# First stage of a pooled-attention and two-MLP kernel: conversion chains, softmax reload and query loads laid out over other steps

## The chip, the cores and the metric

One core of a Trainium2 chip runs the whole program. The metric is the device time of one execution in microseconds (us). Engines are called as the profile calls them: PE (matmul), PEld (its weight loads), DVE, ACT, POOL, and SP, whose queue issues every DMA here.

## The reference, cut to what matters

```python
k_p = k.reshape(B, H, Sp, 8, D).mean(axis=3)      # keys and values pooled by 8: 576 -> 72 rows
v_p = v.reshape(B, H, Sp, 8, D).mean(axis=3)
attn = softmax(q @ k_p.T / sqrt(D))               # B = H = 8, 576 queries, D = 64
x = (attn @ v_p) as 4608 tokens x 512
h = x @ w_in;  x = (h * sigmoid(h)) @ w_out       # first MLP, d_ff 2048
h = x @ w_in2; out = (h * clip(h + 3, 0, 6) / 6) @ w_out2
```

The weights arrive as 64-bit floats and the product must keep more than one 32-bit matmul pass gives. So each weight is converted from its two 32-bit words, and then split into a high part and a remainder (two tiles in the matmul's format).

## The kernel before, in words

Tokens are worked in 9 groups of 512 (`NG`), each of 4 tiles of 128 (`TPG`). The first stage is a loop over 9 groups times 16 blocks of d_ff: step n = 16 g + f. Each step makes one block of h in `h_mm` (12 matmuls of 128x512: high and remainder parts of 4 blocks of depth), and beside it pieces of other chains, at places that tables fix:

- **Attention of a later tile** (table `todo`): `scores`, one step later `all_exps` (row maximum on DVE, eight exponentials with row sums on ACT), later `norm`, then either `probs_T` (group 1: transposes on PE) or `vector_T` (transposes of 32x32 on DVE, then through DRAM: `move` stores the block `bl` and reloads it re-ordered), `weighted` (product with the pooled values) and `split_x` (high part on ACT, remainder on DVE).
- **Conversion of w_in**, in group 0 alone: `split_a` (scale on ACT, shift, merge of the low word and sign on DVE) and `split_b` (high part on ACT, remainder on DVE), called by `conv_a` and `conv_b` after a step's matmuls, about five and four steps ahead of use. For every other weight block (`mul`) the sign is an activation on ACT (L116) and a multiplication on POOL (L125) in place of the third DVE instruction (L127).
- **Factors of later stages** (`pair_jobs`, groups 1 to 8): pairs of weight quarters are loaded (`load_half`), converted (`half_a`), combined on POOL (`combine`), split (`half_b`, tile `hout`) and stored. One job is run per step by `run_job`, 7 jobs a pair, none at f in `REST`.
- **Pooling of keys and values** (`pool_k`, `pool_v`): on POOL, but for the first keys of batch 0 and all of batch 1, which DVE reduces (L336).
- **silu** of the step before: tanh on ACT, one multiply-add on DVE, store of g.

`manual_schedule` keeps each engine's instructions in the order in which the program writes them, so one instruction that waits holds up all behind it on that engine; that goes for SP's queue of DMAs too. In a step the order is: loads, everything in `later` (stores of g and of factors, `move`), silu, `split_x`, softmax, `h_mm`, scores or weighted, conversions or a factor job, norm and turn, pooling. Buffers that matter: 2 for q tiles, 4 PSUM banks for h in turn (so `h_mm(n)` needs the silu of step n - 4), 2 PSUM banks for scores, 3 raw quarters, 4 converted quarters (`mag`), 4 split ones (`out`).

The first stage ends at 559 us; the two later stages are the same code in both kernels.

Of the kernel before, what the change touches and what calls it, by code (L numbers as in the profile page):

```python
# [25 lines left out]
def kernel(  # L26
# [80 lines left out]
    def split_a(f, mul=False):  # L107


        raw = w_raw.pop(f)  # L110
        hw = raw[:, :, 1]
        mag = prep_tile("out", [P, DM], F32)
        bits = mag.bitcast(U32)
        nc.scalar.activation(mag, hw.bitcast(F32), AF.Copy, scale=2.0 ** -112)
        if mul:
            nc.scalar.activation(hw.bitcast(F32), hw.bitcast(F32), AF.Sign)  # L116
        nc.vector.tensor_scalar(
            out=bits, in0=bits, scalar1=3, scalar2=None, op0=ALU.logical_shift_left
        )
        nc.vector.scalar_tensor_tensor(  # L120
            out=bits, in0=raw[:, :, 0], scalar=29, in1=bits,
            op0=ALU.logical_shift_right, op1=ALU.bitwise_or,
        )
        if mul:
            nc.gpsimd.tensor_tensor(out=mag, in0=mag, in1=hw.bitcast(F32), op=ALU.mult)  # L125
        else:
            nc.vector.scalar_tensor_tensor(  # L127
                out=bits, in0=hw, scalar=0x80000000, in1=bits,
                op0=ALU.bitwise_and, op1=ALU.bitwise_or,
            )  # L130
        w_mag[f] = mag

    def split_b(f):

        mag = w_mag.pop(f)
        t = wts.tile([P, 2, DM], F32R, tag=f"i{f}", name="whl")
        nc.scalar.activation(t[:, 0, :], mag, AF.Copy)
        nc.vector.tensor_tensor(out=t[:, 1, :], in0=mag, in1=t[:, 0, :].bitcast(F32), op=ALU.subtract)
        t = t.rearrange("p a (c f) -> p a c f", f=P)
        w_sl[f] = (t[:, 0], t[:, 1])  # L140
# [64 lines left out]
    def factor_jobs():  # L205

        rest = []
        for piece, n in ((2, NF // 2), (0, EARLY)):
            for p in range(n):
                yield from pair_jobs(p, piece, rest)  # L210
        yield None, rest

# [40 lines left out]
    def pair_jobs(p, piece, rest):  # L253
        d, j = divmod(p, 2)
        m = half_mag
        a11, a12, a21, a22 = quarters(p, piece)

        def out(k, key):
            return lambda: half_b(m[key], piece, d, k, j)

        def make(op, to, x, y):
            return lambda: combine(op, m[to], m[x], m[y])

        first, rest[:] = list(rest), [out(1, a12)]
        return [
            (a22, first),
            (a21, [out(3, a22)]),

            (a11, [make(ALU.add, a22, a21, a22), out(4, a22)]),
            (a12, [out(0, a11)]),  # L270
            (None, [make(ALU.subtract, a21, a11, a21), out(6, a21), make(ALU.subtract, a22, a22, a11)]),
            (None, [out(5, a22), make(ALU.subtract, a22, a12, a22)]),
            (None, [out(2, a22)]),
        ]


# [84 lines left out]
    den_t = {}  # L361
    pT_t = {}
    xs = {}

    def load_q(t, tag=None):
        qt = staging(tag, DM) if tag else att.tile([P, DM], F32, tag="q", name="qT")
# [71 lines left out]
    def all_exps(t):  # L438

        mx = att.tile([P, H, 1], F32, tag="mxa", name="mxa")  # L440
# [4 lines left out]
        nc.vector.tensor_scalar(out=mx, in0=mx, scalar1=-ESCALE, scalar2=None, op0=ALU.mult)  # L445
        for h in range(H):
# [41 lines left out]
    def vector_T(t):  # L488
# [12 lines left out]
        def move():  # L501
            nc.sync.dma_start(out=blocks[t % 2], in_=bT)
            rows = blocks[t % 2].rearrange("(i r) j h q -> j r i (h q)", r=Q)
            for j in range(NB):
                n = min(Q, SP - j * Q)
                nc.sync.dma_start(
                    out=pT[j * Q:j * Q + n].rearrange("r i h q -> r i (h q)"), in_=rows[j, :n]
                )

        later.append(move)  # L510
# [256 lines left out]
    with tc.manual_schedule():  # L767
# [16 lines left out]
        for j in range(NPAIR):  # L784
            load_k(1, j, f"o{NF - 8 + j}")
        for j in range(NPAIR):
# [16 lines left out]
        ]  # L803
        conv = list(range(NF))
        done = []

        def conv_a(n, mul):
            for i in range(n):
                if conv:
                    done.append(conv.pop(0))  # L810
                    split_a(done[-1], mul=(i < mul))

        def conv_b(n=9):
            for _ in range(min(n, len(done))):
                split_b(done.pop(0))

# [28 lines left out]
        conv_a(1, 0)  # L845
# [4 lines left out]
        conv_b(1)  # L850
# [4 lines left out]
        conv_a(2, 2)  # L855
        conv_b(1)
        conv_a(2, 2)
        conv_b(1)
        load_ahead(6)

        REST = (0, 3, 6, 13)
        jobs = list(factor_jobs())
        ahead2 = [key for key, _ in jobs if key]
        jobs_b = []
# [11 lines left out]
        def run_job():  # L876

            nonlocal jobs_b
            for job in jobs_b:
                job()  # L880
            key, jobs_b = jobs.pop(0) if jobs else (None, [])
            if key:
                half_a(*key)

        late_silu = []
        pv = {}
        for g in range(NG):
# [3 lines left out]
            for f in range(NF):  # L891
                n = g * NF + f
                load_ahead(2)
                if n == 2:
                    load_q(TPG)
                if g:
                    load_halves()
                while later:
                    later.pop(0)()
                if late_silu:  # L900
                    silu(*late_silu.pop())
                for what, t in todo.get(n, ()):
# [354 lines left out]
```

## Time and profile before

| | us |
|---|---|
| median of 3 runs | 1589.53 (1588.78 to 1590.38) |
| the profiled execution | 1589.21 |
| its span, first to last instruction | 1586.9 |
| PE busy | 1514.5 (95%) |
| DVE / ACT / POOL busy | 1244.2 / 788.9 / 361.2 |

A share of busy time is a mean over stages. The first stage fills the first third of the span, and PE's idle time lies there. Where a view says `x <- y`, x waited and y was what ended the wait.

### The profile page before, as it was taken

Reading aid. Unit: us, or ns where it says so; the run is one execution under the profiler, and the core shown is the slowest. Engines: PE = TensorE matmul, PEld = TensorE weight load, DVE = VectorE, ACT = ScalarE, POOL = GpSimd, SP = SyncE. Lnnn points to the kernel's source line nnn. Section 1 sums busy time; section 2 is a strip of 40 time slices with the busy share of each in tenths; the row PEclk is TensorE's granted clock in tenths of the full one; section 3 lists DMA queues with packets and bytes.
Section 4 is the critical chain, followed back from the end, with each engine's and each line's share of the span. In section 5 each row is a group of like instructions: output and inputs, shape, how many; then the busy total and the mean of one; then the engine's idle time right before and its main releaser. Section 6 shows DMA issues by size and latency. Waiting matters only on the chain.

```text
span 1586.9 us, 31188 instructions
## 1 busy us (share of the span) xinstructions
PE 1514.5 (95%) x11870; PEld 1433.9 (90%) x11870; DVE 1244.2 (78%) x1795; ACT 788.9 (50%) x1689; POOL 361.2 (23%) x405
## 2 busy tenths in 40 slices
PE   7679799899999999999999999999999999999998
PEld 6468688777788899999999999999999999999998
DVE  7776777687677588998888699888885877878776
ACT  5454454445455344444434466776766534334342
POOL 4455144343401000010000044554543000000000
PEclk9789999999999999999999999999999999999999
DMA  9337777787878985555545956666757954444440
GB/s 295 137 91 220 242 256 252 239 267 226 264 263 272 393 299 192 186 190 176 173 133 183 399 187 216 241 216 214 250 197 262 373 220 134 142 150 146 148 149 32
DMA packets 184820, 342.17 MB, mean 216 GB/s; under 512 B 17120, under 2 KB 89696, under 8 KB 184672
## 3 DMA queue, kind: packets, MB, share of 16 engines
q1 hardware_dynamic: 184672, 340.20, 63.1%
q8 instruction: 93, 1.52, 0.4%
q14 instruction: 55, 0.45, 0.1%
HBM read 194.90 MB, written 145.23 MB: 214 GB/s over the span
## 4 chain that ended last, share of the span: by engine, by line
PE 71%; DVE 12%; DMA 9%; ACT 4%; issue 2%; POOL 1%; SPq 1%; ACTq 0%; DVEq 0%; POOLq 0%
PE pl L729 21%; PE pl L713 21%; PE hps L555 11%; PE px L652 9%; PE pz L652 4%; PE py L652 2%; DMA bl<-stage 2%; ACT pr L448 2%; DVE g L569 2%; DVE hmag L172 1%; DMA wraw<-in_moe_w_in_dram 1%; DMA g<-g 1%; DVE go L1098 1%; DMA hraw<-in_moe_w_out_dram 1%; DVE hmag L169 1%
## 5 line engine op out<-in xcount | busy, mean ns | idle before, releaser
L555 PE MATMUL hps<-x,whl 128*128 128x512 f32 x1728 | 402.9, 392 | 9.6 <-ACT x L536 5.6
L555 PEld LDWEIGHTS hps<-x,whl 128*128 128x128 f32 x1728 | 331.7, 195 | 63.5 <-ACT x L536 6.3
L699 ACT ACTIVATE gs<-gr 128x1024 fp32r<-128x1024 f32 x252 | 253.2, 1053 | 262.3 <-issue 109.2
L713 PEld LDWEIGHTS pl<-gs,wst 128*128 128x128 f32 x3024 | 337.8, 192 | 0.1
L729 PE MATMUL pl<-wst,gs 128*128 128x256 f32 x3024 | 337.8, 275 | 0.0
L713 PE MATMUL pl<-gs,wst 128*128 128x256 f32 x3024 | 337.8, 275 | 0.0
L729 PEld LDWEIGHTS pl<-wst,gs 128*128 128x128 f32 x3024 | 337.8, 192 | 0.0
L700 DVE TENSOR_TENSOR gs<-gr,gs 128x1024 fp32r<-128x1024 f32 x252 | 298.0, 1224 | 36.8 <-ACT gs L699 36.2
L652 PE MATMUL px<-xst,wst 128*128 128x256 f32 x1728 | 206.5, 276 | 5.3 <-ACT c L1163 3.4
L652 PEld LDWEIGHTS px<-xst,wst 128*128 128x128 f32 x1728 | 199.3, 192 | 6.7 <-ACT c L1163 4.0
L201 POOL TENSOR_TENSOR hmag<-hmag 128x256 f32<-128x256 f32 x96 | 82.2, 860 | 455.2 <-DVE hout L196 390.0
L692 DVE TENSOR_TENSOR gr<-gr 128x1024 f32<-128x1024 f32 x144 | 169.5, 1218 | 0.0
L448 ACT ACTIVATE pr<-aps,mxa 128x72 f32<-128x72 f32 x256 | 78.1, 330 | 139.1 <-DVE mxa L445 139.1
L196 DVE TENSOR_TENSOR hout<-hmag,hout 128x256 fp32r<-128x256 f32 x152 | 83.4, 556 | 64.2 <-ACT hout L192 60.4
L569 DVE SCALAR_TENSOR_TENSOR g<-g,hps 128x512 f32<-128x512 f32 x144 | 97.1, 675 | 39.1 <-ACT g L568 38.0
L568 ACT ACTIVATE g<-hps 128x512 f32<-128x512 f32 x144 | 85.7, 610 | 67.1 <-PE hps L555 62.1
L629 POOL TENSOR_TENSOR xst<-xr,xst 128x512 fp32r<-128x512 f32 x58 | 81.3, 1402 | 135.5 <-ACT xst L624 131.3
L652 PE MATMUL pz<-xst,wst 128*128 128x256 f32 x864 | 109.3, 276 | 1.4 <-POOL xst L629 0.9
L652 PEld LDWEIGHTS pz<-xst,wst 128*128 128x128 f32 x864 | 102.5, 192 | 2.3 <-POOL xst L629 1.5
L192 ACT ACTIVATE hout<-hmag 128x256 fp32r<-128x256 f32 x152 | 62.7, 420 | 56.6 <-POOL hmag L201 37.0
L399 PE MATMUL aps<-kbd,qT 128*128 128x144 f32 (+1 forms) x288 | 44.5, 311 | 33.0 <-DMA qT<-in_q_dram 16.0
L399 PEld LDWEIGHTS aps<-kbd,qT 128*128 128x128 f32 (+1 forms) x288 | 36.6, 188 | 41.5 <-ACT pr L448 13.0
(87 smaller groups left out, 1515.4 us busy)
## 6 DMA issues: line engine op xcount, KB each, us to landing
gr<-g SPq DMA_DIRECT2D x144, 512.0 KB
ws<-hout SPq DMA_DIRECT2D x152, 256.0 KB
wst<-ws SPq DMA_DIRECT2D x76, 512.0 KB
g<-g SPq DMA_DIRECT2D x144, 256.0 KB
g<-go SPq DMA_DIRECT2D x144, 256.0 KB
hraw<-in_moe_w_out_dram SPq DMA_DIRECT2D x64, 256.0 KB
bl<-stage SPq DMA_DIRECT2D x28, 384.0 KB
stage<-in_k_dram SPq DMA_DIRECT2D x32, 288.0 KB
```

The source lines that it names most:

```text
L196: nc.vector.tensor_tensor(out=t[:, 1], in0=mag, in1=t[:, 0].bitcast(F32), op=ALU.subtract)
L201: nc.gpsimd.tensor_tensor(out=out, in0=a, in1=b, op=op)
L448: nc.scalar.activation(p_t[t][:, a, i], s_t[t][a][:, i], AF.Exp, scale=ESCALE, bias=mx[:, h], accum_out=den_of(t)[:, h],)
L555: nc.tensor.matmul(ps, w[:, c, :], shuffled(x[:, c, :]), start=(c == 0 and n == 0), stop=(c == NKC - 1 and n == 2),)
L568: nc.scalar.activation(in_two(t), dealt(ps), AF.Tanh)
L569: nc.vector.scalar_tensor_tensor(out=in_two(t), in0=in_two(t), scalar=1.0, in1=dealt(ps), op0=ALU.add, op1=ALU.mult)
L652: nc.tensor.matmul(ps[:, j * HW:(j + 1) * HW], w[:, j, a, c, :], shuffled(x[:, b, c, :]), start=(first and j == 0 and n == 0 and c == 0), ...
L692: nc.vector.tensor_tensor(out=to, in0=a, in1=b, op=ALU.subtract)
L699: nc.scalar.activation(t[:, dd, 0], src, AF.Copy)
L700: nc.vector.tensor_tensor(out=t[:, dd, 1], in0=src, in1=t[:, dd, 0].bitcast(F32), op=ALU.subtract)
L713: nc.tensor.matmul(ps[:, c * HW:(c + 1) * HW], w[:, b, c * P:(c + 1) * P], shuffled(t[:, dd, a, i]), start=(dd == 0 and c == 0 and i == 0 ...
L729: nc.tensor.matmul(ps[:, c * HW:(c + 1) * HW], t[:, dd, a, i, c * P:(c + 1) * P], shuffled(w[:, b]), start=(dd == 0 and c == 0 and i == 0 ...
```

## The change

The order of the work within a step of the first stage, and over how many steps a chain is spread:

- **w_in conversion** becomes four functions: `split_scale` (ACT) five steps ahead of use, `split_bits` (three DVE instructions) four steps ahead, `split_head` (ACT) and `split_tail` (DVE) three steps ahead, the tail behind the step's matmuls, the others ahead of them. No block uses the sign activation and the POOL multiplication any more.
- **Softmax**: the maxima (`all_max`) come first in the step, ahead of silu; the exponentials last ahead of the matmuls, behind the conversion's and the factor job's ACT pieces.
- **Factor pairs** take eight slots in place of seven jobs; scale, bits, head and tail of one quarter lie in different slots, ACT and the first DVE pieces ahead of the matmuls, tails and POOL's combinations behind them. They start at step 14 in place of 16, rest at two blocks of a group in place of four, and so end at step 132 (loads start at step 10).
- **Softmax reload**: the store of `bl` (`there`) is issued one step after the turn, as before; its reload (`back`) one step after that for tiles 8 to 11 and two steps after it from tile 12 on. Both stand ahead of the step's other stores.
- **q** has 3 buffers, and is loaded two tiles ahead. Batch 1's keys are pooled by POOL ahead of the loop. Loads of later keys and values move from the end of a step to its start.

```diff
-    def split_a(f, mul=False):
+    def split_scale(f):
+        hw = w_raw[f][:, :, 1]
+        mag = w_mag[f] = prep_tile("out", [P, DM], F32)
+        nc.scalar.activation(mag, hw.bitcast(F32), AF.Copy, scale=2.0 ** -112)
...
+    def split_bits(f):
...
-        if mul:
-            nc.scalar.activation(hw.bitcast(F32), hw.bitcast(F32), AF.Sign)
...
-        if mul:
-            nc.gpsimd.tensor_tensor(out=mag, in0=mag, in1=hw.bitcast(F32), op=ALU.mult)
-        else:
-            nc.vector.scalar_tensor_tensor(
-                out=bits, in0=hw, scalar=0x80000000, in1=bits,
+        nc.vector.scalar_tensor_tensor(
+            out=bits, in0=raw[:, :, 1], scalar=0x80000000, in1=bits,
...
+    def split_head(f):
+        t = w_sl[f] = wts.tile([P, 2, DM], F32R, tag=f"i{f}", name="whl")
+        nc.scalar.activation(t[:, 0, :], w_mag[f], AF.Copy)
+    def split_tail(f):
...
+        def first(i):
+            if i == 0:
+                half_scale(*a22)
+            elif i == 1:
+                half_scale(*a21)
+                half_bits(*a22)
+            elif i == 2:
+                head(3, a22)
+                half_scale(*a11)
+                half_bits(*a21)
...
+        def second(i):
+            if i == 2:
+                tail(3, a22)
+                make(ALU.add, a22, a21, a22)
...
+            elif i == 7:
+                tail(2, a22)
+        return [(first, second, i) for i in range(8)]
...
-        later.append(move)
+        at_slot(n + 1, there)
+        at_slot(n + (2 if t < 3 * TPG else 3), back)
...
+        for j in range(NPAIR):
+            pool_k(1, j, nc.gpsimd)
...
-        REST = (0, 3, 6, 13)
+        REST = (0, 6)
...
-                if g:
+                if n in (0, 1):
+                    load_q(TPG + 1 + n)
+                if n >= NF - 6:
                     load_halves()
+                if n in kv_in:
+                    load_k(*kv_in[n])
+                    load_v(*kv_in[n])
+                for job in due.pop(n, ()):
+                    job()
                 while later:
                     later.pop(0)()
+                for what, t in now:
+                    if what == "soft":
+                        all_max(t)
                 if late_silu:
                     silu(*late_silu.pop())
...
+                if n + 3 < NF:
+                    split_head(n + 3)
+                if n + 4 < NF:
+                    split_bits(n + 4)
+                if n + 5 < NF:
+                    split_scale(n + 5)
+                job = jobs.pop(0) if n >= NF - 2 and f not in REST and jobs else None
+                if job:
+                    job[0](job[2])
+                for what, t in now:
+                    if what == "soft":
                         new_pr(t)
                         all_exps(t)
                 ps = h_mm(g, f)
...
-                        if t + 1 < NTILE:
-                            load_q(t + 1)
+                        if TPG < t + 2 < NTILE and t > TPG:
+                            load_q(t + 2)
...
-                if g == 0:
-                    conv_b()
-                    conv_a(1, f % 2)
-                elif f % 2 == 0 if g == NG - 1 else f not in REST:
-                    run_job()
...
+                if n + 3 < NF:
+                    split_tail(n + 3)
+                if job:
+                    job[1](job[2])
```

PE's own order is the same in both kernels. Three places on the engines beside it, as the program's order lists them (the line numbers of the change are its own; `hout` is the converted weight in group 0, `whl` its split form, `aps` the scores, `mxa` the maxima, `pr` the probabilities):

DVE, group 0, the step in which tile 4's maxima are taken. Before, from a conversion's shift on:

```order
L117 TENSOR_SCALAR hout<-hout 128x512
L120 SCALAR_TENSOR_TENSOR hout<-wraw,hout 128x512
L127 SCALAR_TENSOR_TENSOR hout<-wraw,hout 128x512
L569 SCALAR_TENSOR_TENSOR g<-g,hps 128x512
L442 TENSOR_REDUCE mxa<-aps 128x4 x2
L445 TENSOR_SCALAR mxa<-mxa 128x8
L138 TENSOR_TENSOR whl<-hout,whl 128x512
```

Now, that step from its start:

```order
L474 TENSOR_REDUCE mxa<-aps 128x4 x2
L477 TENSOR_SCALAR mxa<-mxa 128x8
L613 SCALAR_TENSOR_TENSOR g<-g,hps 128x512
L118 TENSOR_SCALAR hout<-hout 128x512
L121 SCALAR_TENSOR_TENSOR hout<-wraw,hout 128x512
L125 SCALAR_TENSOR_TENSOR hout<-wraw,hout 128x512
L137 TENSOR_TENSOR whl<-hout,whl 128x512
```

The maxima moved ahead of silu and of the step's conversion.

ACT at the same place. Before, the exponentials of tile 4 and the next step:

```order
L448 ACTIVATE pr_89,den<-aps,mxa 128x72 x8
L137 ACTIVATE whl<-hout 128x512
L114 ACTIVATE hout<-wraw 128x512
L116 ACTIVATE wraw<-wraw 128x512
L568 ACTIVATE g<-hps 128x512
```

Now the step with tile 4's exponentials:

```order
L612 ACTIVATE g<-hps 128x512
L132 ACTIVATE whl<-hout 128x512
L111 ACTIVATE hout<-wraw 128x512
L484 ACTIVATE pr_89,den<-aps,mxa 128x72 x8
L612 ACTIVATE g<-hps 128x512
```

The high part `whl`, for which DVE's remainder waits, moved from behind the exponentials to ahead of them, and the sign activation is gone.

SP in group 1, around the softmax block of one tile. Before:

```order
L502 DMA bl_101<-stage 128x768
L506 DMA stage<-bl_101 32x4x256 x2
L506 DMA stage<-bl_101 8x4x256
L573 DMA g_1_187<-g 128x2x256
L367 DMA qT<-in_q_dram 128x512
```

Now:

```order
L543 DMA bl_101<-stage 128x768
L617 DMA g_1_187<-g 128x2x256
L199 DMA ws_0_3_161<-hout 128x512
L154 DMA hraw<-in_moe_w_out_dram 128x512
L549 DMA stage<-bl_101 32x4x256 x2
L549 DMA stage<-bl_101 8x4x256
```

Between the store and the reload that waits for it, the stores and the load of the next step moved in.

## Rows read from the trace of the kernel before

**Rows 1.** The page's head

```profile
span 1586.9 us, 31188 instructions
```

**Rows 2.** Windows: us; PE, PEld, DVE, ACT, POOL busy; clock, DMA share, GB/s

```profile
31.00:125.30 94.30, 67.02 (x344) 53.25 (x345) 71.04 (x104) 49.65 (x130) 45.48 (x49) 0.84 0.42 135
125.30:512.20 386.90, 359.91 (x2066) 304.62 (x2065) 284.28 (x614) 188.15 (x714) 126.51 (x188) 0.97 0.77 250
512.20:559.00 46.80, 46.80 (x219) 41.00 (x218) 23.74 (x43) 17.31 (x34) 3.65 (x5) 1.00 1.01 381
```

**Rows 3.** Waits of PE, 31 to 125.3: us in total, times, longest

```profile
PE aps L399 <- ACT pr L448: 7.0, 3, 6.2
PE aps L480 <- DVE pr L469: 6.2, 3, 3.0
PE aps L399 <- DMA qT<-in_q_dram: 4.6, 1, 4.6
...
```

**Rows 4.** Waits of PE, 110 to 560

```profile
PE aps L399 <- DMA qT<-in_q_dram: 11.4, 6, 4.2
PE hps L555 <- ACT x L536: 4.8, 1, 4.8
PE aps L520 <- DMA stage<-bl: 4.5, 2, 2.6
PE aps L399 <- POOL kbd L331: 3.2, 2, 2.2
...
```

**Rows 5.** Timeline of PE: start, duration, work, idle before

```profile
189.86 4.54 PE L555 MATMUL hps<-x,whl 128*128 128x512 f32 x12 [4.78 <-ACT x L536]
...
512.18 46.89 PE L555 MATMUL hps<-x,whl 128*128 128x512 f32 x216
```

**Rows 6.** Waits of all engines, 31 to 125.3

```profile
ACT pr L448 <- DVE mxa L445: 15.0, 4, 6.2
DVE whl L138 <- ACT whl L137: 14.1, 6, 3.2
ACT whl L137 <- POOL hout L125: 12.9, 8, 4.4
```

**Rows 7.** Groups by line: count, busy us, mean ns, idle before

```profile
L125 POOL TENSOR_TENSOR hout<-hout,wraw 128x512 f32<-128x512 f32 x9 | 12.0, 1338 | 53.7 <-ACT g L568 29.4 <-DVE hout L120 22.9 <-ACT whl L137 1.4
...
L336 DVE TENSOR_REDUCE kbd<-stage 64x72 f32<-64x576 f32 x14 | 10.4, 746 | 5.6 <-DMA stage<-in_k_dram 5.5
...
L127 DVE SCALAR_TENSOR_TENSOR hout<-wraw,hout 128x512 uint32<-128x512 uint32 x7 | 7.3, 1040 | 0.2
```

**Rows 8.** Groups by line: pooling of keys on POOL

```profile
L326 POOL TENSOR_TENSOR stage<-stage 128x288 f32<-128x288 f32 x25 | 21.7, 868 | 75.4 <-DMA stage<-in_k_dram 75.4
...
L331 POOL TENSOR_TENSOR kbd<-stage 64x72 f32<-64x72 f32 x50 | 18.2, 364 | 3.4
...
L327 POOL TENSOR_TENSOR stage<-stage 128x144 f32<-128x144 f32 x25 | 12.5, 501 | 2.0
```

**Rows 9.** Timeline of DVE, one instruction alone and one beside POOL

```profile
50.19 0.69 DVE L120 SCALAR_TENSOR_TENSOR hout<-wraw,hout 128x512 uint32<-128x512 uint32 x1
...
55.79 1.64 DVE L120 SCALAR_TENSOR_TENSOR hout<-wraw,hout 128x512 uint32<-128x512 uint32 x1
```

**Rows 10.** Timeline of POOL at that place

```profile
55.43 1.44 POOL L346 TENSOR_TENSOR stage<-stage 72x512 f32<-72x512 f32 x1
```

**Rows 11.** Waits of SP's queue, 125 to 512

```profile
SPq L506 <- DMA bl<-stage: 114.6, 28, 6.6
```

**Rows 12.** Waits of all engines, 125 to 512

```profile
ACT pr L448 <- DVE mxa L445: 124.2, 28, 8.6
...
DVE hout L196 <- ACT hout L192: 59.3, 23, 3.0
```

**Rows 13.** Chain that ended last, in order of time: start, us, what

```profile
126.80 4.54 DMA hraw<-in_moe_w_out_dram
...
422.02 6.16 DMA qT<-in_q_dram
```

More of the change, by code (lines that the diff above doesn't have):

```diff
@@ L203 @@
     EARLY = 5
[L205 to L211, printed above, removed]
     def quarters(p, piece):
@@ L365, in load_q @@
     def load_q(t, tag=None):
[L366 removed]
+        qt = staging(tag, DM) if tag else att.tile([P, DM], F32, tag="q", name="qT", bufs=3)
         nc.sync.dma_start(out=qt, in_=q[t])
@@ L436, in max_exps, with all_max @@
         s_t.pop(t)
-    def all_exps(t):
-        mx = att.tile([P, H, 1], F32, tag="mxa", name="mxa")
+    def all_max(t):
+        mx = mx_t[t] = att.tile([P, H, 1], F32, tag="mxa", name="mxa")
         for a in range(2):
@@ L499, in vector_T, with there, back @@
             )
-        def move():
+        def there():
             nc.sync.dma_start(out=blocks[t % 2], in_=bT)
+        def back():
             rows = blocks[t % 2].rearrange("(i r) j h q -> j r i (h q)", r=Q)
             for j in range(NB):
-                n = min(Q, SP - j * Q)
+                m = min(Q, SP - j * Q)
                 nc.sync.dma_start(
-                    out=pT[j * Q:j * Q + n].rearrange("r i h q -> r i (h q)"), in_=rows[j, :n]
+                    out=pT[j * Q:j * Q + m].rearrange("r i h q -> r i (h q)"), in_=rows[j, :m]
                 )
-        later.append(move)
+        at_slot(n + 1, there)
+        at_slot(n + (2 if t < 3 * TPG else 3), back)
         pT_t[t] = lambda h, o, n: pT[:, o // Q:(o + n) // Q, h, :]
@@ L854 @@
         split_x(3, pv3)
[L855 to L858, printed above, removed]
-        load_ahead(6)
-        REST = (0, 3, 6, 13)
-        jobs = list(factor_jobs())
-        ahead2 = [key for key, _ in jobs if key]
-        jobs_b = []
+        split_bits(1)
+        split_scale(2)
+        split_head(1)
+        split_bits(2)
+        split_tail(1)
+        split_scale(3)
+        split_head(2)
+        split_bits(3)
+        split_tail(2)
+        split_scale(4)
+        load_ahead(6)
+        REST = (0, 6)
+        jobs = []
+        pairs = [(p, 2) for p in range(NF // 2)] + [(p, 0) for p in range(EARLY)]
+        ahead2 = []
+        for p, piece in pairs:
+            jobs += pair_slots(p, piece)
+            ahead2 += [quarters(p, piece)[i] for i in (3, 2, 0, 1)]
         w_need = [(d, k) for k in LAST[2:] for d in range(ND)]
@@ L953 @@
         silu(*late_silu.pop())
-        while jobs or jobs_b:
-            load_halves()
-            run_job()
         while later:
             later.pop(0)()
+        assert not jobs and not ahead2 and not due
         coming = {}
```

120 lines of the change are left out of this document (60 added, 60 removed).

## The prediction

> **What bounds the kernel now.** I read the page's head first, then the windows of the first stage, then who PE waits for in each, then the engines that make it wait. The profiled execution took 1589.21 us, its span 1586.9 [rows 1], so 2.3 us lie around the span; the median of the three runs is 1589.53, 0.3 above, and I sum against 1589.2.
>
> PE's order and matmuls are the same in both kernels, so only its idle time and its clock can change. The windows [rows 2] show where these are. In the last 18 steps of the first stage PE is busy for all of 46.8 us: 216 matmuls in 46.89 us [rows 5], 2.60 us a step, nothing to win. In group 0 (31 to 125.3 us, 16 steps) it is busy 67.0 of 94.3 us at a mean clock of 0.84; in the steps between (125.3 to 512.2) 359.9 of 386.9 at 0.97. The reader is to see that the first stage alone is touched, and that group 0 is far the worst: 5.9 us a step against 2.60.
>
> In group 0 PE waits for exponentials (7.0 us), normalised rows (6.2) and the first q tile (4.6) [rows 3], 17.8 us in these three. After it PE waits for q (11.4), for the high part of x (4.8), for the softmax reload (4.5) and for pooled keys (3.2) [rows 4], 23.9 us. Each long wait costs twice: after the 4.78 us in front of step 32 the next 12 matmuls take 4.54 us [rows 5] in place of 2.60: the pace of the lower of the clock's two levels, 1.2 in place of 2.4 GHz, into which it falls after PE stood. From the windows the clock's loss is at most 0.16 x 94.3 = 15.1 us in group 0 and 0.03 x 386.9 = 11.6 after it. So the ceilings are 17.8 + 15.1 = 33 us in group 0 and 23.9 + 11.6 = 35.5 after it.
>
> **The conversion over three steps (group 0).** DVE is what group 0 waits for: 71.0 us busy in 94.3 [rows 2], and idle for the rest because it and ACT stop each other. ACT's exponentials wait for maxima that stand last in DVE's step (15.0 us), DVE's remainder waits for a high part that stands behind those exponentials on ACT (14.1 us), and ACT's high part waits for POOL's multiplication (12.9 us) [rows 6]. The change cuts all three: maxima first, high part ahead of the exponentials and of the step's matmuls, no multiplication. What it does to DVE's sum: batch 1's eight key reductions go, 8 x 0.746 = 6.0 us; nine blocks get the third instruction, 9 x 1.04 = 9.4 us [rows 7]. 71.0 - 6.0 + 9.4 = 74.4 us. Behind the last conversion stand four silu and one split, 5 of 104 instructions, 5 x 71.0/104 = 3.4 us, which lie beside the last matmuls; so 71 us up to the last remainder, which the step that uses it needs. With DVE never idle that is at 31 + 71 = 102 us, and 2.6 us later group 0 ends: 104.6. I add 3 us for steps in which silu's tanh sits behind a tile's exponentials on ACT, and take 2.4 off (next part): 105 in place of 125.3, a gain of **20 us**. Bounds: if DVE stays as idle as now (71.0 of 94.3, 75%), 71/0.75 = 95 us and no gain; if DVE's collisions vanish, PE's ceiling of 33. I take the value near DVE's sum since its three stops have rows and each has lost its cause. ACT is no bound: 49.65 us of 94.3 [rows 2], less nine sign activations. First w_in blocks: the loads keep their order but for one q tile of 256 KB ahead of the second half, well before step 3 needs them.
>
> **Pooling of batch 1 on POOL.** Added: 4 x (0.868 + 0.501 + 2 x 0.364) = 8.4 us [rows 8] ahead of the loop, where POOL had nothing to do; removed: 12.0 us of multiplications [rows 7]. Scores of tile 4 wait for these keys at the end of step 2; the loads stand where they stood. DVE pays for POOL's time: a merge takes 0.69 us alone and 1.64 beside a POOL addition of 1.44 [rows 9, 10], 0.95 of 1.44, two thirds. POOL's 8.4 - 12.0 = -3.6 us give DVE back two thirds, 2.4 us. The Trainium skill's page SBUF — State Buffer, section Who interferes with whom, says that a DVE instruction with two SBUF inputs and a GpSimd one that reads SBUF lock each other out for a whole instruction. By it the 8.4 us of pooling, which now run beside the loop's first conversions, could hold DVE for all of 8.4 us against the 6.0 of reductions saved there; over the group it gives 3.6 us back in place of 2.4, a sum of 1541. The trace agrees in kind, but [rows 9, 10] show two thirds of an instruction lost, not all of it.
>
> **Softmax order, reload and q (groups 1 to 8).** SP stands 114.6 us in 28 waits for the softmax store before its own reload, up to 6.6 us each [rows 11], with q loads and the next stores queued behind. Now a step lies between (two from tile 12 on), 3.3 us if the 110 steps of this window (386.9 us, 3.5 each) get shorter as forecast; so a wait of 4.1 us in the mean shrinks to about 1 for tiles 8 to 11 and to none after. ACT stands 124.2 us for maxima behind silu, conversions and transposes on DVE, and DVE 59.3 us for high parts behind exponentials [rows 12]; these are the late split of x and the late silu. Of PE's waits [rows 4] I take away: q 11.4, all (a load that lands 6.16 us after issue [rows 13] is now wanted a whole tile later, three steps, 7.8 us or more); x 4.8, all; the reload 2.5 of 4.5, since tiles 8 to 11 keep only two steps between reload and use; keys 1.6 of 3.2, since POOL's combinations still stand ahead of its pooling. That is 20.3. Of the clock's 11.6 I take 8, as most low stretches follow those waits. New waits I put at 1. Gain **27 us**; bounds 0 (DVE late again) and 35.5.
>
> **Factor pairs over eight slots.** No instruction more; they move. New is that the load of a pair's fourth quarter starts when the first is converted in slot 1 and its scale stands on ACT in slot 3: about 1.5 steps, 4.9 us, against a landing of 4.54 [rows 13]. ACT may stand a microsecond per pair, 13 pairs, ahead of exponentials that nobody needs for two steps: nothing on PE's path while four PSUM banks cover it. If that cover goes, it is the rival below. The scale of the next pair's first quarter waits for DVE's last remainder, one step earlier: covered likewise. Half as many pieces fall in the last group, whose DMA share is 1.01 [rows 2]: a relief, no gain since PE is full there. Later stages: no instruction moves, 0.
>
> **Sum.** 1589.2 - 20 - 27 = 1542 us.
>
> **The rivals.**
> - *DVE keeps half of its idle time* (its chains still meet ACT's in each step): group 0 takes 71/0.87 = 82 us and ends at 115, a gain of 10, and half of 27 after it: 24 us, **1565**. For: 75% busy now, and collisions with POOL in every step. Against: each stop of rows 6 lost its cause.
> - *Full relief*: both ceilings, 33 + 35.5 = 68, **1521**. Against: DVE's sum in group 0 allows it only without collisions.
> - *Slower*: raw quarters late. The fourth quarter has 4.9 us from load to use, and the PSUM banks give two steps more, 6.6 us. From a landing of 11.5 us on, each further microsecond stops PE once a pair. With DMAs issued more densely (0.77 busy for 387 us becomes 0.77 x 387/360 = 0.83) a landing of 16 us would cost 13 x 4.5 = 58 us against the gain of 47: **1600**. Against: the longest of rows 13 is 6.16.
> - *It does not do what it says*: DVE as late as now, the wait only under another name; **1589**.
>
> **Chances and range.** Forecast 0.67 (its own range 1528 to 1556), half idle 0.18, full relief 0.07, slower 0.05, no effect 0.03. A measurement of this kernel tells 0.2%, 3.2 us, from no change. Faster 0.92, same 0.03, slower 0.05. The range reaches from below full relief to the half-idle case: 1518 to 1566.
>
> **What would show it.** In the changed profile step 16 starts near 105 us and the last stretch of 18 steps ends near 512 (559 before). DVE in group 0 is busy over 90%. PE's wait for q is gone, also SP's for the softmax store in most of its 28 places, and ACT's 124 us for maxima is under 30. Wrong in the first step: DVE idle in group 0 behind ACT. Wrong in the second: PE waits in groups 1 to 8 of over 10 us, by whatever name. The later stages should take the same 1028 us from 559 to 1587; if they do not, the sum misses a coupling.

## The result, and the profile after

| | before | changed |
|---|---|---|
| median of the runs, us | 1589.15 (4 runs, 1587.10 to 1590.38) | **1544.22** (4 runs, 1541.16 to 1551.74) |
| ratio to before, 95% interval | | **0.9726** (0.9688 to 0.9763) |
| profiled execution, its span | 1589.21, 1586.9 | 1551.74, 1549.7 |
| group 0 ends; last 18 steps begin; first stage ends | 125.3; 512.2; 558.9 | 111.3; 472.6; 519.3 |

The prediction was 1542 us, range 1518 to 1566: faster, by nearly the amount that was forecast. The changed kernel was measured twice more, on two different chips, each time beside the kernel before: 1551.03 against 1590.65 (0.9749, 0.9728 to 0.9769) and 1546.97 against 1591.3 (0.9740, 0.9717 to 0.9762). So the gain is 40 to 45 us, and the experiments below are measured against the middle ratio, 0.974, or, where the changed kernel ran beside them, against its ratio there. The first four ran without it, so their losses are known to about 4 us. The profiled execution is the longest of its four, so its rows show a little less than the gain.

The windows of the changed kernel, cut where group 0, the steps up to the last 18, and the last 18 end (from, to, length; busy time and instructions of PE, PEld, DVE, ACT, POOL; the granted clock; DMA share; GB/s). They answer to [rows 2]:

```profile
31.00:111.30 80.30, 63.79 (x345) 52.07 (x346) 72.58 (x110) 43.64 (x125) 43.91 (x52) 0.87 0.56 180
111.30:472.50 361.20, 353.67 (x2065) 302.11 (x2063) 283.18 (x619) 193.77 (x718) 127.21 (x188) 0.99 0.85 271
```

Group 0 takes 80.3 us in place of 94.3, and DVE is busy for 90% of it in place of 75%. The steps behind it take 361.2 in place of 386.9, PE is busy for 98% of them, and the clock stands at 0.99 in place of 0.97. The last 18 steps and the later stages are what they were, as the matmuls that begin each show (start, length, what, count; they answer to [rows 5]):

```profile
472.55 46.89 PE L599 MATMUL hps<-x,whl 128*128 128x512 f32 x216
519.27 50.97 PE L757 MATMUL pl<-gs,wst 128*128 128x256 f32 x455
```

The waits of PE in the first stage (30 to 560 us; total, times, longest) answer to [rows 3, 4]:

```profile
PE aps L431 <- ACT pr L484: 8.4, 3, 6.7
PE hps L599 <- ACT x L580: 4.6, 2, 2.4
PE aps L564 <- ACT pr L484: 4.2, 2, 3.0
PE hps L599 <- DVE whl L137: 4.0, 4, 1.9
PE aps L564 <- DMA stage<-bl: 2.8, 1, 2.8
PE aps L431 <- POOL kbd L362: 0.7, 1, 0.7
```

No wait for q is left (11.4 us, and 4.6 in group 0, before). The wait for exponentials is the one that has not shrunk: 6.7 us of it is a single stop in group 0. SP's queue between 100 and 480 us and ACT between 105 and 480 us answer to [rows 11, 12]:

```profile
SPq L154 <- DVE hmag L177: 56.0, 32, 4.1
SPq L549 <- DMA bl<-stage: 21.8, 13, 3.9
```
```profile
ACT pr L484 <- DVE mxa L477: 44.0, 23, 5.7
```

The reload stops SP for 21.8 us in 13 places in place of 114.6 in 28, and ACT waits 44.0 us for maxima in place of 124.2. Part of SP's time went over to the raw quarters of w_out (56.0 us for DVE to free their buffers, 24.9 before); ACT waits for raw quarters for 7.7 us (w_in and w_out), and no wait of PE bears their name.

### The profile page after: what moved, and what is told of

It is laid out like the page before. It is cut to its first block, busy times and chain, and to the rows that moved or that the text cites. A ratio compares the mean times of both kernels' runs of the same rounds, so it can differ in the third digit from the quotient of the medians.

```text
span 1549.7 us, 31231 instructions
## 1 busy us (share of the span) xinstructions
PE 1506.2 (97%) x11870; PEld 1430.8 (92%) x11870; DVE 1241.4 (80%) x1796; ACT 786.1 (51%) x1680; POOL 362.2 (23%) x412
## 5 line engine op out<-in xcount | busy, mean ns | idle before, releaser
L599 PE MATMUL hps<-x,whl 128*128 128x512 f32 x1728 | 398.9, 389 | 8.6 <-ACT x L580 4.6
L744 DVE TENSOR_TENSOR gs<-gr,gs 128x1024 fp32r<-128x1024 f32 x252 | 297.7, 1222 | 37.2 <-ACT gs L743 36.7
L696 PEld LDWEIGHTS pz<-xst,wst 128*128 128x128 f32 x864 | 102.6, 192 | 3.1 <-POOL xst L673 2.4
L484 ACT ACTIVATE pr<-aps,mxa 128x72 f32<-128x72 f32 x256 | 78.0, 330 | 46.2 <-DVE mxa L477 46.2
L660 POOL TENSOR_TENSOR xr<-xr 128x512 f32<-128x512 f32 x33 | 46.0, 1394 | 116.2 <-DMA wst<-ws 114.5
L1146 DVE SCALAR_TENSOR_TENSOR go<-go,u 128x512 f32<-128x512 f32 x72 | 62.8, 873 | 4.4 <-ACT go L1143 3.9
```

The lines of the kernel that those rows point to most:

```text
L599: nc.tensor.matmul(ps, w[:, c, :], shuffled(x[:, c, :]), start=(c == 0 and n == 0), stop=(c == NKC - 1 and n == 2),)
L696: nc.tensor.matmul(ps[:, j * HW:(j + 1) * HW], w[:, j, a, c, :], shuffled(x[:, b, c, :]), start=(first and j == 0 and n == 0 and c == 0), ...
L744: nc.vector.tensor_tensor(out=t[:, dd, 1], in0=src, in1=t[:, dd, 0].bitcast(F32), op=ALU.subtract)
```

## Experiments, first: one part of the change undone at a time

In each of these the rest of the change stays. If the parts were worth what the prediction gave them, the five losses would add up to the gain.

**q one tile ahead, two buffers, as before.**

```
-        qt = staging(tag, DM) if tag else att.tile([P, DM], F32, tag="q", name="qT", bufs=3)
+        qt = staging(tag, DM) if tag else att.tile([P, DM], F32, tag="q", name="qT")
...
-                        if TPG < t + 2 < NTILE and t > TPG:
-                            load_q(t + 2)
+                        if t + 1 < NTILE:
+                            load_q(t + 1)
```

> The change with q tiles loaded one tile ahead in two buffers, as before. Theory A (the reload apart from its store freed the SP queue, and q was only late because it stood behind it): time within 5 us of the changed kernel's 1544 us, PE waits under 4 us for q. Theory B (the distance of two tiles is what took PE's wait for q away): 11 to 18 us slower, 1555 to 1562, and PE waits for q again by some 10 us.

1556.26 us (1554.67 to 1561.51), ratio 0.9788 (0.9768 to 0.9807): some 8 us slower than the changed kernel. PE's waits in the first stage:

```profile
PE aps L431 <- DMA qT<-in_q_dram: 5.2, 1, 5.2
PE aps L431 <- DVE hmag L177: 4.8, 1, 4.8
```

Both rows are waits for q. The second carries DVE's name, since the view names what signalled last; the stop itself and the load of q that it needed, as SP issued it, are

```profile
390.30 2.19 PE L431 MATMUL aps<-kbd,qT 128*64 128x144 f32 x16 [4.84 <-DVE hmag L177]
385.85 0.40 SPq L399 DMA_DIRECT2D qT<-in_q_dram  x1
```

The trace has the last part of that load landing at 390.17 us, 0.13 before PE goes on; PE's stop at 130.76 ended 0.14 behind the landing of its q tile too. The scores use nothing that L177 makes, and the DVE work that they do need, the maxima of the tile before, was over by 382.6 us. So 10.0 us of waiting for q come back, in two places, of the 11.4 in six that the kernel before had: theory B in the waits. The 8 us of time lie between the two theories.

**The reload right behind its store, as before.**

```
-        at_slot(n + (2 if t < 3 * TPG else 3), back)
+        at_slot(n + 1, back)
```

> The change with the softmax block's reload issued right behind its store. Theory A (SP's wait for the store is the root of the waits after group 0): SP waits some 115 us for the store again and the time is 12 to 25 us above the changed kernel's 1544. Theory B (q two tiles ahead and the other orders cover a late SP): SP waits as long, but the time is within 5 us of 1544.

1576.37 us (1573.85 to 1577.74), ratio 0.9908 (0.9895 to 0.9921): 27 us slower, the largest of the five, on theory A's side and a little above its range. SP's queue (100 to 500 us), and ACT (105 to 500 us):

```profile
SPq L549 <- DMA bl<-stage: 127.9, 28, 6.6
```
```profile
ACT g L612 <- DMA g<-g: 55.4, 18, 7.5
ACT pr L484 <- DVE mxa L477: 31.4, 16, 5.7
ACT hmag L164 <- DMA hraw<-in_moe_w_out_dram: 24.3, 5, 9.2
```

All 28 places are back. What stands behind them in SP's queue is late: the stores of g, for whose buffers the next tanh waits (55.4 us, 2.2 in the changed kernel and 2.8 in the kernel before), and the raw quarters (24.3). ACT waits less for maxima than in the changed kernel. Group 0 is not longer than there: its step 14 starts at 102.5 us (106.0). The loss lies behind it: the steps from 107.8 to 498.9 us take 391.1 us in place of 361.2, and PE waits for 27.5 us there in place of 7.6, by six names, none of them q. So q two tiles ahead is early enough even with a late SP. And the wait for the stores of g is one that the kernel before hardly had: a part undone in the changed kernel does not only bring back what it cost before.

**The maxima behind the silu, the conversions and the split, as before.**

```
                 now = todo.get(n, ())
-                for what, t in now:
-                    if what == "soft":
-                        all_max(t)
...
                     if what == "soft":
+                        all_max(t)
                         new_pr(t)
```

> The change with a tile's maxima taken where they stood, behind silu, split and conversions and right ahead of the exponentials. Theory A (ACT's stand for the maxima made the chains late): ACT waits over 100 us for maxima again, 8 to 20 us slower than 1544, most of it in group 0. Theory B (ACT has room, only the total of DVE counts): ACT waits, but the time is within 4 us of 1544.

1574.01 us (1572.94 to 1574.67), ratio 0.9893 (0.9879 to 0.9906): 24 us slower. ACT (105 to 500 us) and PE (30 to 560 us):

```profile
ACT pr L484 <- DVE mxa L477: 81.2, 23, 8.4
```
```profile
PE aps L431 <- ACT pr L484: 19.2, 11, 7.3
```

The wait for maxima nearly doubles, and PE stands 19.2 us for exponentials in place of 8.4. Step 14 starts at 114.9 us, 9 later, so a third of the loss is in group 0. Theory A has the sign, but it expected over 100 us of ACT's waiting, at most 20 us of time, and most of it in group 0.

**Conversions of w_in and pooling of batch 1 as before.**

```
-                if n + 3 < NF:
-                    split_head(n + 3)
-                if n + 4 < NF:
-                    split_bits(n + 4)
-                if n + 5 < NF:
-                    split_scale(n + 5)
...
+                if g == 0:
+                    conv_b()
+                    conv_a(1, f % 2)
```

> The change with group 0's conversions and batch 1's pooling as before (two pieces, sign by ACT and POOL on every other block, keys reduced on DVE). Theory A (the conversion's three steps made the 14 us that group 0 won in the profile): group 0 ends some 14 us later, time 1556 to 1562. Theory B (group 0 won by q tile 4 being early and the maxima being first): group 0 ends within 5 us of the changed kernel's, time 1544 to 1549.

1559.31 us (1555.92 to 1561.98), ratio 0.9806 (0.9792 to 0.9819): 10 us slower. Step 14 starts at 115.57 us (106.01 in the changed kernel, 120.05 before), so the loss is that of group 0, and some 4 of the 14 us that group 0 gained would come from the rest of the change; that is no more than the start of step 14 spreads between profiles (see the fourth part).

**Factor pairs in four conversions each, spread as before.**

```
-        REST = (0, 6)
+        REST = (0, 3, 6, 13)
...
-                job = jobs.pop(0) if n >= NF - 2 and f not in REST and jobs else None
...
+                if g and (f % 2 == 0 if g == NG - 1 else f not in REST):
+                    run_job()
```

> The change with the factor pairs' seven jobs, their places and their rests as before. Theory A (a quarter's whole conversion in one step and its high part behind the exponentials made DVE and ACT stop each other in groups 1 to 8): 6 to 15 us slower than the changed kernel's 1544, DVE waits for high parts some 50 us again. Theory B (softmax order and reload suffice, the pairs hide behind PE): within 4 us of 1544.

1554.62 us (1551.45 to 1559.1), ratio 0.9785 (0.9767 to 0.9803), beside 0.9749 (0.9728 to 0.9769) for the changed kernel beside it: 6 us by the ratios, 3.6 by the medians, and the intervals just touch, so the loss is likely, but no more than that. The prediction had priced this part at nothing. What does change clearly are the waits of ACT and SP (ACT from 105, SP from 100 to 480 us):

```profile
ACT pr L454 <- DVE mxa L447: 87.9, 26, 7.1
```
```profile
SPq L154 <- DVE hmag L177: 82.2, 36, 5.9
```

They are double and one and a half times what the changed kernel has (44.0 and 56.0). The likely reason, which no run separates, is that with all of a quarter's DVE work in one step the next step's maxima come later. The steps from 107.3 to 472.9 us take 365.6 us in this profile, 361.2 and 361.8 in the changed kernel's first two; group 0 ends 4 us earlier than in the first of them, which is within its spread.

**What the five say together.** 8 + 27 + 24 + 10 + 6 = 75 us of losses against a gain of 41. The parts do not add. One reason that fits is that waits of before had causes that lay beside one another, so that leaving one of them keeps a good part of the time; another is that a part undone here makes stops that the kernel before did not have, as the stores of g show. How much of the 34 us each makes up, no run tells.

## Experiments, second: one part alone

**The kernel before, with the reload apart from its store and nothing else.**

```
-        later.append(move)
+        at_slot(n + 1, there)
+        at_slot(n + (2 if t < 3 * TPG else 3), back)
```

> The kernel before with one part of the change alone: the reload of a tile's softmax blocks is issued a step (from tile 12 on, two steps) behind its store, in place of right behind it. Theory A (the reload that waits for its own store holds the raw quarters of w_out and the g stores behind it in SP's queue, and that is a cost by itself): the 114.6 us of SP in front of the reload fall under 40, PE's waits for q and bl and x in groups 1 to 8 shrink by about 8 us together, and with the clock's share the time is 10 to 15 us lower, about 1577. Theory B (the links hang together: with the pairs still made four steps in a row and q one tile ahead, the queue that is freed only waits at the next link): SP's wait moves to the raw quarters behind DVE, PE's q waits stay near 11 us, and the time is under 6 us lower, 1585 or more.

1589.4 us (12 runs, 1582.83 to 1593.57) against 1591.3, ratio 0.9984 (0.9969 to 0.9999). Theory B: the part that costs 27 us when it is undone brings about 2.5 (0 to 5) when it is done alone. SP's queue, 100 to 500 us, first of the kernel before and then of this one:

```profile
SPq L506 <- DMA bl<-stage: 114.6, 28, 6.6
SPq L153 <- DVE hmag L176: 24.1, 21, 4.0
```
```profile
SPq L153 <- DVE hmag L176: 101.7, 40, 6.6
SPq L513 <- DMA bl<-stage: 11.6, 6, 3.1
```

The wait for the reload nearly goes, as it should, and SP waits almost as long (101.7 us) in front of the next raw quarter, for whose buffer DVE has not finished. ACT still waits 122.7 us for maxima in this profile. PE's waits for q (110 to 560 us) seem to shrink:

```profile
PE aps L399 <- DVE den L468: 6.3, 1, 6.3
PE aps L399 <- DMA qT<-in_q_dram: 1.9, 1, 1.9
```

But the 6.3 us, and 0.6 more under another name of DVE, end 0.13 to 0.14 us behind the landing of a q tile, as above, and scores use nothing of either. So 8.9 us of q are left of 11.4: with q one tile ahead, its wait stays whether the reload stands apart or not. That the queue was one limit and the order of DVE's and ACT's steps another of about the same height, so that whoever removes one meets the other, fits this; no run removes the second alone from the kernel before.

## Experiments, third: group 0 and the pooling

The changed kernel was run again beside these, as it is:

> The changed kernel once more, for a second profile and the scatter of its executions (1541 to 1552 so far, the profiled one being the longest). If the scatter lies in group 0, the last stretch of 18 steps starts at another time than 472.5 us but 361 us behind group 0's end; if it lies in the later stages, that start stays within 2 us.

1551.03 us (1544.67 to 1551.78), the ratio 0.9749 that was given above. The profile's last 18 steps start at 473.68 us, 361.8 behind the end of group 0 at 111.9.

**Batch 1 pooled with one addition in place of three.**

```
-        if eng:
+        if eng and b != 1:
             eng.tensor_tensor(out=t[:, :, 0:4], in0=t[:, :, 0:4], in1=t[:, :, 4:8], op=ALU.add)
```

(and the same for V)

> The change without the first two of the three additions that pool batch 1's keys and values (their pooled rows are not the sums): some 14 us less of POOL between 28 and 60 us. Theory A (DVE sets group 0 and POOL stretches it by about 0.3 us for each of its own): DVE's last remainder 4 to 5 us earlier, time 1537 to 1541. Theory B (a DVE instruction is locked out for all of POOL's): 10 us or more, under 1535. Theory C (PE and ACT set group 0 there): within 2 us of 1544.

1539.3 us (1538.96 to 1541.94), ratio 0.9687 (0.9673 to 0.9701): 12 us below the changed kernel beside it, more than theory A expected and as much as theory B did, though the time itself is in theory A's range. PE's steps 14 and 15, here and in the first profile of the changed kernel:

```profile
96.29 5.45 PE L600 MATMUL hps<-x,whl 128*128 128x512 f32 x24
```
```profile
106.01 5.45 PE L599 MATMUL hps<-x,whl 128*128 128x512 f32 x24
```

So most of it is in group 0. Between 31 and 109 us POOL works for 25.1 us here and for 43.9 in the changed kernel. Up to the end of the last remainder (here 94.05 us, there 103.7) DVE's and POOL's busy time is, first here and then there:

```profile
31.00:94.05 63.05, 53.51 (x299) 43.87 (x300) 61.24 (x102) 40.91 (x118) 22.77 (x30) 0.92 0.61 200
31.00:103.70 72.70, 56.19 (x299) 45.72 (x300) 68.82 (x103) 40.95 (x120) 40.98 (x48) 0.86 0.55 180
```

DVE is busy for 7.6 us less and idle for 2.1 less, which together are the 9.7. PE waits for no pooled rows in group 0 of either profile, so it is not that these come earlier. In the changed kernel POOL works from 28.5 to 60.2 us with hardly a pause. Operations of conversions on DVE in that time and behind it:

```profile
38.14 1.02 DVE L118 TENSOR_SCALAR hout<-hout 128x512 uint32<-128x512 uint32 x1
45.01 1.77 DVE L137 TENSOR_TENSOR whl<-hout,whl 128x512 fp32r<-128x512 f32 x1
48.72 1.63 DVE L125 SCALAR_TENSOR_TENSOR hout<-wraw,hout 128x512 uint32<-128x512 uint32 x1
62.57 0.42 DVE L118 TENSOR_SCALAR hout<-hout 128x512 uint32<-128x512 uint32 x1
63.75 0.69 DVE L125 SCALAR_TENSOR_TENSOR hout<-wraw,hout 128x512 uint32<-128x512 uint32 x1
```

The four operations of a conversion take, as means over the 16 slices of group 0 (27 to 103 us):

```profile
L125 DVE SCALAR_TENSOR_TENSOR hout<-wraw,hout 128x512 uint32<-128x512 uint32 x16 | 14.6, 913 | 0.5
L137 DVE TENSOR_TENSOR whl<-hout,whl 128x512 fp32r<-128x512 f32 x16 | 14.6, 912 | 0.0
L121 DVE SCALAR_TENSOR_TENSOR hout<-wraw,hout 128x512 uint32<-128x512 uint32 x16 | 13.8, 863 | 0.5
L118 DVE TENSOR_SCALAR hout<-hout 128x512 uint32<-128x512 uint32 x16 | 10.3, 641 | 0.8 <-ACT hout L111 0.8
```

Against 0.69, 0.68, 0.69 and 0.42 us when alone, that is 16 x (0.22 + 0.23 + 0.17 + 0.22) = 13.6 us, beside 43.9 us of POOL: 0.31 us of DVE for each us of POOL (0.9 of the 13.6 stand in operations beside which POOL did nothing). The light pooling gave DVE 7.6 us back for 18.2 of POOL, 0.42. So the price here is 0.3 to 0.4.

**Batch 1's keys reduced on DVE, as before.**

```
-        for j in range(NPAIR):
-            pool_k(1, j, nc.gpsimd)
...
+                if n < 2:
+                    for j in (2 * n, 2 * n + 1):
+                        pool_k(1, j)
```

> The change with batch 1's keys reduced on DVE in steps 0 and 1 as before. Theory A (0.3 us of DVE for each us of POOL): DVE pays 6.0 us and saves about 3, so 2 to 4 us slower than 1544. Theory B (locked out for whole instructions): DVE saves 8 us or more and the kernel is 2 us or more faster.

1550.55 us (1548.72 to 1552.88), ratio 0.9755 (0.9739 to 0.9772), beside 0.9749 for the changed kernel: no difference that can be measured. DVE takes on the reductions, and POOL's work beside it falls. This is its row for the two blocks of four:

```profile
47.95 3.04 DVE L367 TENSOR_REDUCE kbd<-stage 64x72 f32<-64x576 f32 x4
54.01 3.04 DVE L367 TENSOR_REDUCE kbd<-stage 64x72 f32<-64x576 f32 x4
```

Between 31 and 109 us DVE is busy for 73.9 us in place of 70.9: of the 6.0 us that it takes on, 3.0 come back for 10.2 us less of POOL (33.7 for 43.9), as theory A has it. But the 2 to 4 us of time that theory A adds do not show: step 14 starts at 106.75 us, and at 106.58 in the changed kernel's profile beside it. Why not stays open; PE's stops in the first stage change places (8.5 us for keys on DVE, and 4.0 for exponentials in place of 10.1). So moving 6 us of reductions from DVE to POOL freed half of it on DVE, and no time.

## Experiments, fourth: what is left, and a version that is faster

**Other steps for the attention of group 2.**

```
-            w, back = NF + (6, 9, 11, 14)[i], 7
+            w, back = NF + (7, 10, 12, 13)[i], (8, 8, 8, 7)[i]
```

> The changed kernel with other steps for the attention of group 2: weighted products at steps 23, 26, 28 and 29 in place of 22, 25, 27 and 30, eight steps behind the scores (seven for the last tile) in place of seven. Theory A (what is left in groups 1 to 8 is two late links, tile 8's reload that is waited for 2.75 us at 138 us, with 2.35 us of low clock behind it, and tile 11's split that step 32 waits 2.44 us for at 175 us, with 1.7 us of low clock behind it): both waits go, and the time is 7 to 9 us lower than the changed kernel's, a ratio to before near 0.970 where the control of this call has 0.974. Theory B (the reload is late because SP and the rings are full then, so a later use is only waited for at another tile): the waits move to tiles 9 to 11, and the time is within 3 us of the control.

**The same, and the scores of tile 5 in two PSUM banks of their own.**

```
-                        scores(t)
+                        scores(t, [(ps_y, "y2"), (ps_y, "y3")] if t == 5 else A)
```

> The kernel with the other steps for group 2, and with the scores of tile 5 in the two PSUM banks y2 and y3, which are free in step 4, in place of the banks that tile 4's exponentials still read. Theory A (PE stands 6.74 us at 60 us for those banks, but DVE sets the end of group 0): the wait goes or shrinks below 1 us, PE waits for remainders in its place, the last product of step 14 still starts at 103 to 106 us, and the time is within 3 us of the kernel with the other steps alone. Theory B (the banks tie PE to DVE's step and so make group 0 end late): group 0 ends 4 to 7 us earlier, step 14 starts at 99 to 102 us, and the time falls by as much.

**The changed kernel for the third time, beside these.**

> The changed kernel again, as it is, for a comparison on this chip. Theory A (the spread between its runs of 1541 and 1552 us is of the runs and not of the chip): both kinds of times appear, 1541 to 1547 and 1549 to 1552, and the median is anything between. Theory B (the chip sets it): the times of this call lie within 3 us of each other.

The three gave 1543.23 us (1540.12 to 1546.09; ratio 0.9701, 0.9680 to 0.9723), 1540.57 (1539.22 to 1542.76; **0.9690**, 0.9671 to 0.9708) and 1546.97 (1545.95 to 1553.56; 0.9740, 0.9717 to 0.9762). The one with both edits is faster than the changed kernel: the intervals do not meet, and the medians stand 6.4 us apart.

The other steps bring about 4 to 6 us of the 7 to 9 expected, but their interval and that of the changed kernel overlap, so alone they are not told apart from no gain. The two stops that the edit aimed at, in the changed kernel:

```profile
138.42 1.97 PE L564 MATMUL aps<-stage,vp 72*64 72x128 f32 x16 [2.75 <-DMA stage<-bl]
140.32 5.21 PE L599 MATMUL hps<-x,whl 128*128 128x512 f32 x12
175.65 4.54 PE L599 MATMUL hps<-x,whl 128*128 128x512 f32 x12 [2.44 <-ACT x L580]
```

and what stands in that stretch with the edit:

```profile
148.33 1.09 PE L564 MATMUL aps<-stage,vp 72*64 72x128 f32 x16 [1.33 <-DMA stage<-bl]
157.29 1.09 PE L564 MATMUL aps<-stage,vp 72*64 72x128 f32 x16 [1.50 <-DMA stage<-bl]
162.83 1.09 PE L564 MATMUL aps<-stage,vp 72*64 72x128 f32 x16 [1.66 <-DVE hmag L170]
```

Both stops are gone, the 12 matmuls at the low clock behind each (5.21 and 4.54 us where 2.6 is the rule) too; three shorter ones have come at tiles 9 to 11 (the third, under DVE's name, ends 0.14 us behind a landing of the reload too). So both theories hold in part.

The banks of tile 5 were expected to matter not at all or by 4 to 7 us. The stop, in the changed kernel, and what took its place:

```profile
60.28 2.54 PE L431 MATMUL aps<-kbd,qT 128*128 128x144 f32 x8 [6.74 <-ACT pr L484]
```
```profile
70.12 1.89 PE L516 MATMUL aps<-ident,pr 128*72 128x128 f32 x8 [6.15 <-DVE pr L505]
```

The scores no longer wait, and PE stands as long 10 us later for tile 4's normalised rows, which come from DVE. The two kernels' times differ by 2.7 us, and their intervals overlap. Step 14 starts at 101.66 us against 104.80, but it starts anywhere from 101.8 to 106.6 in the seven profiles whose conversions, pooling and softmax in group 0 are the same, so this one does not tell either. That the banks are worth up to 3 us stays open. The moved wait and the time speak for theory A, that they are not what sets group 0; the start at 101.66 lies where theory B had it, so it is not settled.

The third measurement has times from 1545.95 to 1553.56 on one chip: the spread of the changed kernel is of its runs, not of the chip. It goes with the granted clock. Of its 13 runs, those at a mean granted clock of 0.992 or above took 1541 to 1547 us, those at 0.987 to 0.990 took 1551 to 1554 (the three at 0.991 lie between 1546 and 1551).

## Why the prediction was right, and where it was wrong

**Sum.** 47 us forecast, 45 in the first comparison, 40 and 44 in the others. That the first comes within 2 us of the forecast is in part luck: the runs of one kernel spread over 12 us, and group 0 gave less than its term. In the spans of the profiled executions: group 0 ends 14.0 us earlier, the steps up to the last 18 take 25.7 less, the last 18 the same, and the later stages 1030.4 in place of 1028.0, so 37.2 in all. In the profile of the third measurement the three terms are 14.8, 28.2 and 0.1: 43.1.

**Group 0: 14 to 15 us in place of 20.** The failing step is "With DVE never idle that is at 31 + 71 = 102 us, and 2.6 us later group 0 ends". Its first half held. DVE stood still for 2.4 us in all, and the last remainder began at 103.00:

```profile
103.00 0.68 DVE L137 TENSOR_TENSOR whl<-hout,whl 128x512 fp32r<-128x512 f32 x1
```

The second half did not: 7.6 us pass from that remainder's end to the end of group 0, in this profile and in those of both repetitions. The layout makes the last remainder three steps ahead of its use, so PE never waits for it. PE's last stop in group 0 is for softmax, and from there it works without a pause:

```profile
90.11 1.09 PE L564 MATMUL aps<-stage,vp 72*64 72x128 f32 x16 [1.15 <-ACT pr L484]
```

Six matmul steps with the attention that lies between them take the 21.2 us from 90.1 to 111.3. PE had lost 6.7, 3.0 and 1.2 us to exponentials by then, which follow DVE's maxima, and 4.0 in four stops to earlier remainders. So of the 6.3 us between 105 and 111.3, 5.0 are this step (7.6 for 2.6), 1.1 are DVE's own lateness (103.7 for 102 + 3 - 2.4 = 102.6), and 0.2 is rounding. Seven profiles with the same conversions, pooling and softmax end group 0 between 107 and 112 us, a gain of 13 to 18 us; so this term lay above all of them.

**DVE's collisions with POOL.** The prediction took two thirds of POOL's time from one pair of rows [rows 9, 10]. Over group 0 it is 0.3 to 0.4. POOL's time was off too: its additions for batch 1's keys took 11.5 us between 28.5 and 41.1, not 8.4, so POOL's busy time in group 0 fell by 1.6 us (45.5 to 43.9) and not by 3.6. The term falls from 2.4 us to about 0.5, a small one here; but the light pooling shows what the price can buy: 18 us less of POOL made group 0 some 10 us shorter. The rule from the Trainium skill's page SBUF — State Buffer, section Who interferes with whom (a DVE instruction with two SBUF inputs and a GpSimd one that reads SBUF lock each other out), agrees in kind: a remainder of 0.68 us took 1.77 at its worst, beside a POOL addition. Taken as a loss for all of POOL's time, which is an estimate, it would give 43.9 us, and DVE lost 13.6. The forecast's own terms for the keys alone, 6.0 us saved on DVE and two thirds of 8.4, 5.6, lost to POOL, come to nothing, and so did the time with the keys back on DVE; on DVE the move freed 3.0 us.

**Groups 1 to 8: 25.7 to 28 us for 27.** The sum over PE's waits and the clock was right, and PE's waits there are 7.6 us by all names, under the 10 that would have refuted it. PE's idle time fell by 19.5 us (27.0 to 7.5) and its busy time by 6.2 (359.9 to 353.7), for 19.3 and 8 in the sum. The clock stands at 0.99, and the two stretches of 12 matmuls shown above at its lower level lie behind a stop. The term for q held by itself: with q one tile ahead 10.0 us of its wait come back, with the reload apart and nothing else 8.9 stay, and with q two tiles ahead none is left even behind a late SP. What was wrong is the price of two other parts: the factor pairs were priced at nothing and probably hold 4 to 6, and the reload was priced at 2.5 and costs 27 when it is undone with all else in place, though it brings 2.5 when nothing else is. The prediction added up PE's idle time, which is why its total held, while not all of its parts did. SP's wait for the store is gone in 15 of its 28 places, just most of them.

**Maxima on ACT.** Under 30 us was forecast for the 124.2 behind group 0, and 44.0 was measured; over the whole run it is 46.2 against 139.1:

```profile
L484 ACT ACTIVATE pr<-aps,mxa 128x72 f32<-128x72 f32 x256 | 78.0, 330 | 46.2 <-DVE mxa L477 46.2
```

The maxima now come first in DVE's step, but DVE probably enters a step late when the one before was full. After 180 us PE waits for nothing up to the end of the stage, so from there on what is left of it costs nothing.

**Rivals.** Raw quarters were not late: no wait of ACT for one is longer than 1.1 us from w_out in the changed kernel up to 480 us (4 waits, 3.0 us together), and one of 4.7 us for a quarter of w_in is all that stands beside them. DVE did not keep half of its idle time (it was busy for 90% of group 0), and full relief was kept from group 0 by DVE's sum.

## What to carry to other kernels

Where several engines take turns in one step, the waits of a profile have causes that lie beside one another: price the idle time of the engine that bounds the stage, not each cause by the wait that bears its name, and test a part both by undoing it in the changed kernel and by doing it alone, for here the same part read 27 us one way and 2.5 the other. The name on a wait is a guess at what came last: three waits for q stood under DVE's name here, and only the landing of the load told. A load that must wait for its own store should not stand right behind it in an in-order queue; what it delays is everything queued after it, and the profile puts that down to other names. Work that is moved to an idle engine is not free if the two engines hold each other up: moving 6 us of reductions from DVE to POOL here freed 3.0 us of DVE and changed nothing in the time.

## What was not expected of the hardware

- DVE's 128x512 operations take 0.42 and 0.69 us when POOL is idle and up to 1.50 and 1.77 beside POOL's additions, and a POOL addition of one shape takes between 1.26 and 1.81 us in that stretch; over group 0 DVE lost 0.3 to 0.4 us for each us that POOL worked, about half of what one pair of rows had said.
- The changed kernel scatters more than the one before, 0.8% (1541 to 1554) against 0.5% (1586 to 1594, over all measurements), with its clock. Why some runs get a mean of 0.995 and others 0.988 in the same program was not settled; the two profiles at 0.987 and 0.988 begin their last 18 steps 3.4 and 4.5 us later than the one at 0.991, and take 1.4 to 2.5 us more in the later stages.
